# Scores of windowed and strided attention as products on quarters of the array, ahead of two expert layers

## The chip, the cores and the metric

The kernel runs on one core of one Trainium2 chip. The metric is device time in microseconds (us), from the first instruction of the program to the last. Three runs of the kernel before took 961.97, 963.13 and 961.53 us, with a median of 961.97.

TensorE (PE) multiplies a stationary operand, loaded by a weight load (PEld), with a moving operand, and writes to PSUM, which has eight banks. VectorE (DVE) and ScalarE (ACT) read PSUM and write SBUF, GpSimd (POOL) works on SBUF alone, and SyncE (SP) issues the transfers. Each engine runs its own list of instructions in order and waits on semaphores for the others.

## The reference

All of it is float32. Four batches of 576 tokens, eight heads of 64: heads 0 to 3 look at the last 32 positions, heads 4 to 7 at every position with the same remainder by 32. Then two expert layers follow, which make up most of the arithmetic.

```
scores = (q @ k.T) / 8                       # B=4, H=8, S=576, D=64
rel    = pos[:, None] - pos[None, :]
local   (heads 0-3): 0 <= rel < 32
strided (heads 4-7): rel >= 0 and both positions equal mod 32
attn   = softmax(where(mask, scores, -1e9)) @ v
x      = attn, tokens by 512                 # 2304 tokens
x      = (h - tanh(h)) @ w_out               # h = x @ w_in, 512 -> 2048 -> 512
xn     = x / rms(x) * rms_g
out    = (silu(xn @ w_gate) * (xn @ w_val)) @ w_out2      # 512 -> 1536 -> 512
```

## The kernel before, in words

The tokens are cut into nine sub-blocks, numbered `j`. Sub-blocks 0 to 3 are positions 0 to 255 of the four batches, sub-block 4 holds the last 64 positions of all four, and 5 to 8 are positions 256 to 511. They are worked in five groups, (0,1), (2,3), (4), (5,6), (7,8), with 512 columns each, 256 for the middle one. The attention of one group runs while the first expert layer of the group before it runs. For the first group there is nothing to run beside, so the program begins with attention alone.

The first expert layer has 16 steps `f`. Each step makes `ps_h` (12 products of 128 rows by 128 columns of weights, moving up to 512 columns), takes the hyperbolic tangent on ACT (`tg`), makes `g` as a high and a low part on DVE and ACT, and adds 12 products to `ps_x`. The weights come as 64-bit numbers: one weight tile is loaded as `raw` (512 KB), turned into a float by one ACT or POOL instruction (`ca`) and three of DVE (`ct`), and split into a high and a low part (`w`). `st1` walks through the weights `in 0, in 1, out 0, in 2, out 1, ...`. The second expert layer follows the same pattern with `ps_h`, `ps_m` and `ps_x`, and its weights are turned while the last group of the first layer runs.

Attention on a sub-block goes in two units of 128 rows of scores, in stages:

- `st_s`: scores into `ps_s`, then the softmax. For heads 0 to 3 (class `Local`), 64 queries of two heads form one product: the queries lie in `qz`, 128 rows by 128 columns with two blocks of zeros, so that one product on the whole array gives both heads, against 96 keys in `kT`. Four products make a unit. The first 64 positions of a batch have no keys ahead of them and use 64 keys (`wide`).
- `st_p`: the weights of the softmax are transposed on PE (`ps_p`) and copied to `pT`.
- `st_v`: the products with the values, into `ps_v`, and the copy into the expert layer's input `xs`, a high part on ACT and a low one on DVE.

Heads 4 to 7 go the same way in class `Dense` for all sub-blocks but 4: positions of equal remainder lie together, 64 keys (`k_den`, sub-blocks 0 to 3) or 128 (`k_far`, sub-blocks 5 to 8), with the queries in `qd`, zeros included. In `st_v` it makes 16 products of 32 columns, in an order of the head's numbers that the rows of `w_in` are sorted to. In sub-block 4 class `Strided` computes heads 4 to 7 with products on POOL and sums on DVE, and turns the result on DVE (`fin`, L531).

For sub-block 0 the stages draw PSUM tiles from two pools in turn, `ps_m` and `ps_h`, with two tiles each; for all later ones from `ps_m` alone, since `ps_h` belongs to the expert layer. A stage `st_s` takes one tile.

What sets the order: the string `START` names the first steps one by one (letters a to e and A to E load inputs of sub-blocks 0 and 1, `t` the masks, `w` loads a weight, `s` turns one, a digit is one stage of that sub-block, `U` is a step of the expert layer). After that the stages are spread over the steps. This gives the order in which the program is written; a scheduler then places each instruction on its engine's list by when it reckons the inputs to be ready, so lists can differ from the written order.

## Time and profile before

| | us |
|---|---|
| median of three runs | 961.97 |
| the profiled execution, its own time | 962.53 |
| its span, first instruction to last | 960.8 |
| PE busy | 929.7 (97%) |
| DVE busy | 519.9 (54%) |
| ACT busy | 346.5 (36%) |
| POOL busy | 119.6 (12%) |

The chain of work that ended last, followed back from the last instruction, is PE for 78% of the span, DVE for 11%, transfers for 5%. By tile, `ps_h`, `ps_x` and `ps_m` of the expert layers are 30%, 30% and 14%; `ps_s`, `ps_v` and `ps_p` of the attention are 2%, 2% and 1%.

How to read the rows below: a table by stretch gives, for each stretch of time, the busy time of PE, PEld, DVE, ACT and POOL with the number of instructions in brackets, then the granted clock of PE as a share of 2.4 GHz, the busy share of the transfer engines and what they moved. A row in order of time gives the start, the busy time, the engine, the line, the instruction, its operands (tile sizes of the array, then partitions by columns), how many of them are merged, and in square brackets how long the engine had idled before and for whom. Products overlap, so their cost on the path is read from start to start, not from the busy time. A float32 product appears as two instructions, so the four products of a unit's scores are "x8"; a transpose is one.

### The profile page before, as it was taken

The numbers are of one execution on the slowest core, as the hardware profiler recorded it, in microseconds if no ns is written. First come the engines' busy times: TensorE is split into PE (matmuls) and PEld (weight loads), VectorE is DVE, ScalarE is ACT, GpSimd is POOL, SyncE is SP. The second block draws the span as 40 slices with busy tenths as digits, with TensorE's granted clock in tenths as the row PEclk, the third lists the DMA queues.
The fourth block names the chain that finished last, engine by engine and source line by source line (L and its number), as shares of the span: only waits on it lengthen the run. The fifth ranks groups of instructions, "written<-read, shape, count | busy, mean of one in ns | idle before, by whom it ended". The sixth has DMA issues, their size and how long they took to land.

```text
span 960.8 us, 13712 instructions
## 1 busy us (share of the span) xinstructions
PE 929.7 (97%) x5274; PEld 779.3 (81%) x5274; DVE 519.9 (54%) x1199; ACT 346.5 (36%) x820; POOL 119.6 (12%) x147
## 2 busy tenths in 40 slices
PE   5799999999999999999899999999999999999998
PEld 5688888888999888887667778888888888888897
DVE  4899998873454433269999764254124412331212
ACT  4776654223554433244445323113111311121211
POOL 2000036760000000013334210000000000000000
PEclk9799999999999999999999999999999999999999
DMA  9936334220421200066335211101010000000100
GB/s 204 336 127 209 109 104 141 77 79 1 122 84 42 77 31 1 23 219 200 129 105 181 71 39 44 44 1 44 1 44 1 23 1 33 11 1 1 43 2 23
DMA packets 51489, 72.66 MB, mean 76 GB/s; under 512 B 24928, under 2 KB 35552, under 8 KB 51424
## 3 DMA queue, kind: packets, MB, share of 16 engines
q1 hardware_dynamic: 51424, 71.80, 24.5%
q8 instruction: 41, 0.67, 0.3%
q14 instruction: 24, 0.20, 0.1%
HBM read 62.34 MB, written 9.44 MB: 75 GB/s over the span
## 4 chain that ended last, share of the span: by engine, by line
PE 78%; DVE 11%; DMA 5%; issue 3%; POOL 1%; SPq 1%; ACT 1%; POOLq 0%; ACTq 0%
PE ps_h L111 30%; PE ps_x L111 30%; PE ps_m L111 14%; PE ps_s L111 2%; DVE ct L139 2%; DVE ct L142 2%; DVE ct L138 2%; PE ps_v L111 2%; DMA raw<-in_w_out_dram 2%; DVE w L151 1%; DMA raw<-in_w_val_dram 1%; DVE g L662 1%; PE ps_p L325 1%; DMA qz<-in_q_loc_dram 1%; DMA x<-x2d 1%
## 5 line engine op out<-in xcount | busy, mean ns | idle before, releaser
L111 PE MATMUL ps_h<-xs,w 128*128 128x512 f32 (+1 forms) x984 | 220.9, 369 | 6.2 <-DVE tg L651 6.0
L111 PE MATMUL ps_x<-g,w 128*128 128x512 f32 (+1 forms) x984 | 222.0, 368 | 0.6 <-DVE g L662 0.5
L111 PEld LDWEIGHTS ps_h<-xs,w 128*128 128x128 f32 x984 | 169.7, 190 | 37.9 <-DVE tg L651 9.2
L111 PEld LDWEIGHTS ps_x<-g,w 128*128 128x128 f32 x984 | 168.5, 188 | 31.4 <-DVE g L662 1.9
L111 PE MATMUL ps_x<-w,p 128*128 128x512 f32 x648 | 158.9, 392 | 3.5 <-DVE p L766 2.2
L111 PE MATMUL ps_m<-xn,w 128*128 128x512 f32 (+1 forms) x720 | 158.4, 368 | 0.8 <-DVE xn L745 0.8
L111 PE MATMUL ps_h<-xn,w 128*128 128x512 f32 (+1 forms) x720 | 159.0, 369 | 0.1
L763 DVE SCALAR_TENSOR_TENSOR s<-ps_m,s 128x512 f32<-128x512 f32 (+1 forms) x60 | 38.2, 637 | 221.6 <-PE ps_m L111 219.3
L111 PEld LDWEIGHTS ps_h<-xn,w 128*128 128x128 f32 x720 | 126.8, 188 | 24.8 <-DVE tg L651 0.4
L111 PEld LDWEIGHTS ps_m<-xn,w 128*128 128x128 f32 x720 | 126.0, 188 | 24.3 <-DVE xn L745 1.2
L111 PEld LDWEIGHTS ps_x<-w,p 128*128 128x128 f32 x648 | 120.4, 188 | 30.6 <-DVE p L766 3.5
L651 DVE SCALAR_TENSOR_TENSOR tg<-ps_h,tg 128x512 f32<-128x512 f32 (+1 forms) x82 | 50.9, 620 | 86.5 <-ACT tg L646 86.5
L762 ACT ACTIVATE s<-ps_h 128x512 f32<-128x512 f32 (+1 forms) x60 | 33.3, 555 | 158.9 <-PE ps_h L111 158.9
L646 ACT ACTIVATE tg<-ps_h 128x512 f32<-128x512 f32 (+1 forms) x82 | 44.5, 543 | 98.0 <-PE ps_h L111 94.3
L765 ACT CAST p<-s 128x512 fp32r<-128x512 f32 (+1 forms) x60 | 34.6, 577 | 124.1 <-DVE s L763 124.1
L657 ACT CAST g<-tg 128x512 fp32r<-128x512 f32 (+1 forms) x82 | 46.6, 569 | 51.5 <-DVE tg L651 51.4
L662 DVE TENSOR_TENSOR g<-tg,g 128x512 fp32r<-128x512 f32 (+1 forms) x82 | 55.3, 674 | 16.9 <-ACT g L657 16.6
L150 ACT CAST w<-ct 128x512 fp32r<-128x512 f32 x68 | 42.1, 620 | 45.0 <-DVE ct L142 42.5
L766 DVE TENSOR_TENSOR p<-s,p 128x512 fp32r<-128x512 f32 (+1 forms) x60 | 38.7, 645 | 25.8 <-ACT p L765 25.6
L139 DVE SCALAR_TENSOR_TENSOR ct<-ca,ct 128x512 uint32<-128x512 uint32 x68 | 52.1, 767 | 0.7
L142 DVE SCALAR_TENSOR_TENSOR ct<-raw,ct 128x512 uint32<-128x512 uint32 x68 | 51.7, 761 | 0.4
L131 ACT ACTIVATE ca<-raw 128x512 f32<-128x512 f32 x50 | 33.7, 674 | 35.1 <-DVE ct L139 18.0
(89 smaller groups left out, 723.1 us busy)
## 6 DMA issues: line engine op xcount, KB each, us to landing
raw<-in_w_out_dram SPq DMA_DIRECT2D x28, 512.0 KB, 5.8
raw<-in_w_in_dram SPq DMA_DIRECT2D x16, 512.0 KB, 8.7
raw<-in_w_gate_dram SPq DMA_DIRECT2D x12, 512.0 KB, 4.0
raw<-in_w_val_dram SPq DMA_DIRECT2D x12, 512.0 KB, 3.8
x2d<-xe SPq DMA_DIRECT2D x36, 128.0 KB, 1.9
x<-x2d SPq DMA_DIRECT2D x16, 256.0 KB, 4.2
out_dram<-o SPq DMA_DIRECT2D x16, 256.0 KB, 2.0
v<-in_v_loc_dram SPq DMA_DIRECT2D x14, 192.0 KB, 2.6
```

The costliest lines, as they stand in the source:

```text
L111: nc.tensor.matmul(out_, lhsT, rhs, start=start, stop=stop, skip_group_check=True)
L131: nc.scalar.mul(out=a, in_=hi.bitcast(F32), mul=2.0 ** -111)
L139: nc.vector.scalar_tensor_tensor(out=t, in0=a, scalar=0x80000000, in1=t, op0=ALU.bitwise_and, op1=ALU.bitwise_or)
L142: nc.vector.scalar_tensor_tensor(out=t, in0=lo, scalar=29, in1=t, op0=ALU.logical_shift_right, op1=ALU.bitwise_or)
L150: nc.scalar.copy(out=t[:, 0], in_=self.b)
L646: nc.scalar.activation(out=t, in_=h_of[g, f, a], func=ACTF.Tanh, scale=WS)
L651: nc.vector.scalar_tensor_tensor(out=t, in0=h_of.pop((g, f, a)), scalar=WS, in1=t, op0=ALU.mult, op1=ALU.subtract)
L657: nc.scalar.copy(out=t[:, 0], in_=t_of[g, f, a])
L662: nc.vector.tensor_tensor(out=t[:, 1], in0=t_of.pop((g, f, a)), in1=t[:, 0].bitcast(F32), op=ALU.subtract)
L763: nc.vector.scalar_tensor_tensor(out=s, in0=r[1], scalar=WS, in1=s, op0=ALU.mult, op1=ALU.mult)
L765: nc.scalar.copy(out=t[:, 0], in_=s)
L766: nc.vector.tensor_tensor(out=t[:, 1], in0=s, in1=t[:, 0].bitcast(F32), op=ALU.subtract)
```

## The change

- `Local.load_qk` and `Dense.load_qk`: the queries are loaded without zeros, by one transfer of 128 partitions in place of two of 64. The zero fills on POOL and DVE go.
- `st_s` of both: each head is a product of its own, on 64 rows by 64 columns of the array (a quarter). A unit has eight such products in place of four whole ones. Head `hh` of a pair uses rows `64*hh` and up, and has a PSUM tile of its own, so that a stage takes two tiles. The softmax of both classes is one function.
- The keys and values of heads 0 to 3 get 32 positions of zeros in front on the host, so that all units have 96 keys; a second mask, `mask0`, hides them. `wide` and `parts` go.
- `Dense.st_v` makes 8 products of 64 columns in place of 16 of 32, in natural head order, and the rows of `w_in` are no longer sorted.
- `Strided.fin`: four products with the identity into a PSUM tile (`ps_o`) take the place of the DVE transpose. `PR`, the size of a POOL piece, goes from 256 to 384 columns.
- `START` is another string.

```diff
-START = 'dt0AB0w00100ss100w1CDsbEU101w10csw1a1sw110w0Usw1s1e'
+START = 'tabcdewABCDEw0000s0000s0000wU1111s111s1U111s11U1'
...
-    PR = 4 * 64
+    PR = 6 * 64
...
+    def softmax(ps, sm, nm, ss, m):
+        for hh in range(2):
+            for p in range(2):
+                nc.vector.tensor_tensor_reduce(
+                    out=sm[:, hh, p], in0=ps[hh][:, p], in1=m, scale=-scale, scalar=3.0e38,
+                    op0=ALU.add, op1=ALU.min, accum_out=nm[:, hh, p:p + 1],
+                )
...
         def load_qk(self):
...
-                for hh in range(2):
-                    r = slice(64 * hh, 64 * hh + 64)
-                    nc.sync.dma_start(
-                        out=self.qz[r, x0 // 64:(x0 + n) // 64, :, r].rearrange("r u p t -> r (u p) t"),
-                        in_=q_loc[b, r, t0 // 32:(t0 + n) // 32, :],
-                    )
+                nc.sync.dma_start(
+                    out=self.q[:, x0 // 64:(x0 + n) // 64].rearrange("r u p t -> r (u p) t"),
+                    in_=q_loc[b, :, t0 // 32:(t0 + n) // 32, :],
+                )
...
         def st_s(self, i, ps_pool, ps_tag):
...
-            for u in us:
-                for p in range(2):
-                    w = self.wide(u)
-                    mm(
-                        ps[:, u - us[0], p, :w], self.qz[:, u, p, :],
-                        self.kT[:, p, self.at[u] + 96 - w:self.at[u] + 96], True, True,
-                    )
+            for p in range(2):
+                for k, u in enumerate(us):
+                    for hh in range(2):
+                        r = slice(64 * hh, 64 * hh + 64)
+                        mm(
+                            ps[hh][64 * k:64 * k + 64, p, :], self.q[r, u, p, :],
+                            self.kT[r, p, self.at[u]:self.at[u] + 96], True, True,
+                        )
...
         def st_v(self, i, ps_pool, ps_tag):
...
-                for h in range(4):
-                    r = slice(64 * (h % 2), 64 * (h % 2) + 64)
-                    for n in range(2):
-                        a = 64 * h + 32 * n
-                        mm(ps[32 * h:32 * h + 32, n, g], self.v[:, 2 * i + g, a:a + 32], pT[:, g, h // 2, r], True, True)
+                    for hh in range(2):
+                        a = 64 * (2 * p + hh)
+                        mm(
+                            ps[64 * hh:64 * hh + 64, p, g, :], self.v[:, 2 * i + g, a:a + 64],
+                            pT[:, hh, p, 64 * g:64 * g + 64], True, True,
+                        )
...
             def fin(g0, gn):
...
-                    nc.vector.transpose(
...
+                    lanes = ident.rearrange("k (p h l) -> k h p l", p=2, h=2)
+                    for c in range(gn):
+                        for hh in range(2):
+                            mm(ps[64 * hh:64 * hh + 64, :, c, :], self.o[:, c, :], lanes[:, hh], True, True)
```

Where instructions stand, before and after, at three places.

First, SP's list at the start of the program, before. `qz` and `qd` are queries, `kT` and `kd` keys, `v` and `vd` values, `raw` a weight tile.

```order
L258 DMA v<-in_v_loc_dram 96x2x256
L799 DMA tab<-in_tabs_dram 128x416
L240 DMA qz<-in_q_loc_dram 64x8x64 x2
L246 DMA kT<-in_k_loc_dram 128x2x256
...
L382 DMA kd<-in_k_den_dram 128x512
L124 DMA raw<-in_w_in_dram 128x512
L240 DMA qz<-in_q_loc_dram 64x8x64
...
L378 DMA qd<-in_q_den_dram 64x8x64
L124 DMA raw<-in_w_in_dram 128x512
L124 DMA raw<-in_w_out_dram 128x512
```

The same list after the change; the lines left out are the rest of sub-blocks 0, 1 and 2, in this order.

```order
L758 DMA tab<-in_tabs_dram 128x512
L255 DMA ql<-in_q_loc_dram 128x512
L260 DMA kT<-in_k_loc_dram 128x2x288
...
L353 DMA vd<-in_v_den_dram 64x1024
L123 DMA raw<-in_w_in_dram 128x512
L255 DMA ql<-in_q_loc_dram 128x512
...
L353 DMA vd<-in_v_den_dram 64x1024
L123 DMA raw<-in_w_in_dram 128x512
L255 DMA ql<-in_q_loc_dram 128x512
...
L123 DMA raw<-in_w_out_dram 128x512
```

The masks moved to the front, the first weight from behind one and a half sub-blocks to behind one, and the first `w_out` from behind 5136 KB to behind 6112 KB (summed over the rows of the two lists).

Second, ACT's list at the start of the program, before; `sm,ss<-sm,nm` is the exponential of the softmax.

```order
L794 ACTIVATE warm<-warm 128x1
L304 ACTIVATE sm,ss<-sm,nm 128x64 x2
L304 ACTIVATE sm,ss<-sm,nm 128x96 x2
L408 ACTIVATE sm,ss<-sm,nm 128x64 x4
...
L328 COPY pT<-ps_p 96x256
L131 ACTIVATE ca<-raw 128x512
```

The same list after the change.

```order
L753 ACTIVATE warm<-warm 128x1
L130 ACTIVATE ca<-raw 128x512
L223 ACTIVATE sm,ss<-sm,nm 128x96 x4
L223 ACTIVATE sm,ss<-sm,nm 128x64 x4
L223 ACTIVATE sm,ss<-sm,nm 128x96 x4
L223 ACTIVATE sm,ss<-sm,nm 128x64 x4
```

The first weight's `ca` moved from behind 16 exponentials and two copies to ahead of all of them.

Third, PE's list in the middle group's expert layer, where the first unit of sub-block 6 makes its scores, before.

```order
L111 MATMUL ps_x<-g,w 128x256 x11
L111 MATMUL ps_s<-kT,qz 128x96 x4
L111 MATMUL ps_x<-g,w 128x256
L111 MATMUL ps_h<-xs,w 128x256
L111 MATMUL ps_s<-kd,qd 128x128 x4
L111 MATMUL ps_h<-xs,w 128x256 x11
```

The same place after the change, with the numbers of the tiles; the two `ps_s` of a stage are the two heads of a pair.

```order
L110 MATMUL ps_s_2999<-kT_2835,ql_2834 64x96 x4
L110 MATMUL ps_x_2780<-g_2969,w_833 128x256 x3
...
L110 MATMUL ps_h_3108<-xs_1750,w_911 128x256 x12
L110 MATMUL ps_x_2779<-g_3048,w_900 128x256 x3
L110 MATMUL ps_s_3000<-kT_2835,ql_2834 64x96 x4
L110 MATMUL ps_s_3023<-kd_2864,qd_2862 64x128 x4
L110 MATMUL ps_x_2780<-g_3048,w_900 128x256 x3
...
L110 MATMUL ps_h_3163<-xs_1750,w_988 128x256 x10
L110 MATMUL ps_s_3024<-kd_2864,qd_2862 64x128 x4
L110 MATMUL ps_h_3163<-xs_1750,w_988 128x256 x2
```

Two stretches of whole products among the expert layer's became three of quarter products: the two halves of a stage, one for each tile, now stand apart.

## Rows read from the trace of the kernel before

**Rows 1.** By stretch: busy us of each engine (instructions), clock, transfer share, GB/s.

```profile
0.00:10.00 10.00, 2.18 (x10) 2.21 (x11) 0.70 (x5) 1.49 (x2) 5.89 (x15) 1.00 0.75 180
10.00:20.00 10.00, 8.72 (x43) 8.36 (x41) 6.12 (x53) 7.15 (x40) 0.00 (x0) 1.00 1.20 229
20.00:30.00 10.00, 6.26 (x119) 5.23 (x118) 7.14 (x32) 6.26 (x21) 0.00 (x0) 0.84 1.08 296
30.00:40.00 10.00, 7.71 (x46) 7.40 (x47) 8.34 (x28) 7.64 (x27) 0.00 (x0) 0.65 1.05 264
40.00:50.00 10.00, 9.33 (x142) 7.99 (x140) 9.73 (x20) 7.16 (x16) 0.00 (x0) 1.00 1.02 407
50.00:100.00 50.00, 49.83 (x351) 42.06 (x349) 48.60 (x127) 34.89 (x89) 1.04 (x2) 1.00 0.52 169
300.00:350.00 50.00, 50.00 (x351) 42.30 (x349) 23.52 (x88) 23.77 (x74) 1.05 (x2) 1.00 0.21 57
```

**Rows 2.** In order of time, PE at the start: start, busy us, what, count, idle.

```profile
7.82 3.70 PE L111 MATMUL ps_s<-kT,qz 128*128 128x64 f32 x16 [7.82 <-DMA kT<-in_k_loc_dram]
...
33.96 3.40 PE L111 MATMUL ps_h<-xs,w 128*128 128x256 f32 x13
```

**Rows 3.** In order of time, ACT at the start: first exponential, first `ca`, third `ca`.

```profile
10.11 0.35 ACT L304 ACTIVATE sm<-sm,nm 128x64 f32<-128x64 f32 x1 [7.89 <-DVE nm L296]
...
20.08 0.67 ACT L131 ACTIVATE ca<-raw 128x512 f32<-128x512 f32 x1
...
28.82 0.66 ACT L131 ACTIVATE ca<-raw 128x512 f32<-128x512 f32 x1 [1.13 <-DMA raw<-in_w_out_dram]
```

**Rows 4.** In order of time, DVE: the last input column of sub-block 1.

```profile
47.42 0.64 DVE L446 TENSOR_TENSOR xs<-ps_v,xs 128x256 fp32r<-128x256 f32 x1
```

**Rows 5.** By stretch, as rows 1: two stretches of heavy transfers.

```profile
8.00:14.00 6.00, 6.00 (x29) 6.00 (x30) 2.44 (x23) 2.02 (x11) 0.00 (x0) 1.00 1.19 190
24.00:28.00 4.00, 2.66 (x58) 2.18 (x59) 2.68 (x13) 1.91 (x9) 0.00 (x0) 0.85 1.01 386
```

**Rows 6.** In order of time, PE: expert products undisturbed, then four transposes, twice.

```profile
78.84 2.88 PE L111 MATMUL ps_h<-xs,w 128*128 128x512 f32 x12
81.56 1.98 PE L111 MATMUL ps_x<-g,w 128*128 128x512 f32 x8
...
87.01 0.60 PE L325 MATMUL ps_p<-tab,sm 128*96 128x128 f32 x4
87.45 0.60 PE L425 MATMUL ps_p<-tab,sm 128*64 128x128 f32 x4
```

**Rows 7.** In order of time, PE: scores of one unit among expert products.

```profile
361.56 1.03 PE L111 MATMUL ps_s<-kT,qz 128*128 128x96 f32 x8
362.37 2.33 PE L111 MATMUL ps_x<-g,w 128*128 128x512 f32 x9
364.53 2.89 PE L111 MATMUL ps_h<-xs,w 128*128 128x512 f32 x12
367.26 1.05 PE L111 MATMUL ps_s<-kd,qd 128*128 128x128 f32 x8
```

**Rows 8.** In order of time, PE: products with values among expert products.

```profile
382.78 2.88 PE L111 MATMUL ps_h<-xs,w 128*128 128x512 f32 x12
385.59 0.69 PE L111 MATMUL ps_v<-pT,v 96*64 96x64 f32 x16
386.20 3.02 PE L111 MATMUL ps_x<-g,w 128*128 128x512 f32 x12
389.06 2.88 PE L111 MATMUL ps_h<-xs,w 128*128 128x512 f32 x12
391.87 0.69 PE L111 MATMUL ps_v<-pT,vd 128*32 128x64 f32 x32
```

**Rows 9.** In order of time, PE: values with 64 keys, then 96, in one visit.

```profile
67.12 0.83 PE L111 MATMUL ps_v<-pT,v 64*64 64x64 f32 x16
67.88 0.73 PE L111 MATMUL ps_x<-g,w 128*128 128x512 f32 x2
```

**Rows 10.** By group: shape, count; busy us, mean ns; idle before, for whom.

```profile
L296 DVE CUSTOM_DVE_ANT_0 sm<-ps_s,tab 128x96 f32<-128x96 f32 x64 | 12.9, 253 | 2.4 <-PE ps_s L111 2.3
```

More of the change, by code (lines that the diff above doesn't have):

```diff
@@ L212, in copy @@
         return nc.scalar.copy
+    def softmax(ps, sm, nm, ss, m):
[7 more added lines that the diff above has]
+            for p in range(2):
+                nc.scalar.activation(
+                    out=sm[:, hh, p], in_=sm[:, hh, p], func=ACTF.Exp, scale=-1.0,
+                    bias=nm[:, hh, p:p + 1], accum_out=ss[:, hh, p:p + 1],
+                )
+        nc.vector.tensor_scalar_add(out=ss, in0=ss, scalar1=1.0e-9)
+        nc.vector.reciprocal(out=ss, in_=ss)
+        nc.vector.tensor_tensor(
+            out=sm, in0=sm, in1=ss.unsqueeze(3).to_broadcast(list(sm.shape)), op=ALU.mult
+        )
     class Local:
@@ L310, in st_s @@
[L310 to L314 removed]
+            softmax(ps, sm, nm, ss, m)
             self.sm[i] = sm
         def st_p(self, i, ps_pool, ps_tag):
[L318 removed]
             ps = ps_pool.tile([128, 512], F32, tag=ps_tag, name="ps_p")[0:96].rearrange(
[L320 removed]
+                "k (h p t) -> k h p t", h=2, p=2)
@@ L321, in st_p @@
             sm = self.sm.pop(i)
-            for u in range(nu):
+            for hh in range(2):
                 for p in range(2):
-                    w = self.wide(self.units[i][u])
-                    nc.tensor.transpose(ps[:w, u, p, :], sm[:, u, p, :w], ident)
-            pT = room(self.j, att, "pT", tag="pT")[0:96, :512].rearrange("k (u p t) -> k u p t", u=2, p=2)
-            for a, e, w in self.parts(i):
-                copy(self.j, 2 * i)(out=pT[:w, a:e], in_=ps[:w, a:e])
+                    nc.tensor.transpose(ps[:, hh, p, :], sm[:, hh, p, :], ident)
@@ L336, in st_v @@
             pT, v = self.pT.pop(i), self.v.pop(i)
-            for u in range(nu):
+            for u in range(2):
                 for p in range(2):
@@ L968, in lay_out @@
     r2 = row % 64
+    first = near & ((row >= 64) | (col >= 32))
     same = (r2 // 8 == c2 // 8) & (c2 <= r2)
@@ L971, in lay_out @@
     far = (r2 // 8 == c3 // 16) & (c3 % 16 <= 8 + r2 % 8)
-    near, same, far = (_np.where(m, 0.0, -BIG) for m in (near, same, far))
-    tabs = _np.concatenate([near, same, _np.eye(128), far], axis=1).astype(_np.float32)
+    masks = [_np.where(m, 0.0, -BIG) for m in (near, first, same, far)]
+    tabs = _np.concatenate(masks + [_np.eye(128)], axis=1).astype(_np.float32)
+    kp, vp = (_np.pad(a[:, :4], ((0, 0), (0, 0), (32, 0), (0, 0))) for a in (k, v))
     laid = dict(
         q_loc=q[:, :4].reshape(B, 2, 2, S // 64, 64, D).transpose(0, 2, 5, 3, 1, 4).reshape(B, 128, S // 32, 64),
-        k_loc=k[:, :4].reshape(B, 2, 2, S, D).transpose(0, 2, 4, 1, 3).reshape(B, 128, 2, S),
-        v_loc=v[:, :4].transpose(0, 2, 1, 3).reshape(B, S, 4 * D),
+        k_loc=kp.reshape(B, 2, 2, S + 32, D).transpose(0, 2, 4, 1, 3).reshape(B, 128, 2, S + 32),
+        v_loc=vp.transpose(0, 2, 1, 3).reshape(B, S + 32, 4 * D),
         q_str=lanes(q), k_str=lanes(k), v_str=lanes(v),
```

191 lines of the change are left out of this document (66 added, 125 removed).

## The prediction

> **What bounds the kernel now.** I read the table by stretch first. From 50 us on PE is busy without a gap, 49.83 of 50 us and then 50.00 of 50 [rows 1], and the chain that ended last is PE for 78% of the span. So after the start each nanosecond that PE spends more or less on attention moves the end by as much. DVE counts too until 100 us (48.60 of 50), later not (23.52 of 50) [rows 1].
>
> The start is another matter. In the first 50 us PE is idle for 15.8 us and in part of 20 to 40 us runs at the lower of its two clocks (1.2 GHz; granted share 0.84 and 0.65) [rows 1]. DVE is idle for 18.0 us in the same time (10 less each busy figure) [rows 1]. The transfer engines are full from 10 to 50 us [rows 1]. PE's first expert product starts at 33.96 us [rows 2], after a chain that passes the landing of the first `w_out`: ACT waited 1.13 us for it and began its `ca` at 28.82 us [rows 3], so it landed at about 28.4 (the start less some 0.4 us that such a chain shows between landing and start). The attention input of sub-block 1 is complete after the DVE row at 47.42 us [rows 4]; from there on PE and DVE are both full.
>
> So the forecast has two terms: the start, which waits for transfers and for DVE, and the rest, where PE's time counts.
>
> **The start.** The change loads fewer small pieces: queries come in pieces of 2 KB, not of 256 B. The stretch from 8 to 14 us, where queries with zeros, keys and values land, moves 190 GB/s at a full transfer share; the stretch from 24 to 28 us, with weights, moves 386 [rows 5]. But more stands ahead of the first `w_out` on SP's list, 6112 KB in place of 5136, since three whole sub-blocks now come first. What had moved by 28.4 us before is 180 x 10 + 229 x 10 + 296 x 8.4, 6.6 MB [rows 1]; 5648 KB with `w_out` itself are 5.8 MB, so 0.8 MB of later transfers had run beside them. After, 6624 KB (6.8 MB) and again 0.8 MB make 7.6 MB. Transfers begin to move at about 2 us (180 GB/s over 10 us [rows 1] is most of the steady rate). At 386 GB/s `w_out` lands at 21.7 us, at the mean rate of before (232 GB/s over 28.4 us) at 33; I take 300, between the two rows of 5 and near the 296 of 20 to 30 us [rows 1], since the pieces are now 1 to 2 KB for sub-blocks and 4 KB for weights: 27.3 us, 1.1 us earlier.
>
> Two things stand against a larger gain. ACT's list now has `ca` of the first weight ahead of all exponentials, so ACT waits for that weight, and the 16 exponentials of sub-block 0, the copies behind them and DVE's reciprocals wait with it. Before, the first exponential began at 10.11 us and this `ca` at 20.08 [rows 3]. Now 1952 + 512 KB (2.5 MB) are ahead, some 10 to 11 us at 300 GB/s with a start at 2, and the exponentials follow. The first scores can begin about 2 us before the 7.82 us of rows 2, since masks, queries and keys come first, but this gain ends at that wait. Second, behind `w_out` comes as much work of DVE as before: up to the last input of sub-block 1 DVE's list holds the same seven weights begun and five finished. So I carry the 1.1 us through as 1.0 us, with bounds from -6.7 us (386 GB/s) to +4.6 (232 GB/s).
>
> The zero fills on POOL are hidden now (POOL is idle after 10 us) and their removal is worth nothing beyond this. The first two units of each kind use 96 keys in place of 64, four columns of the softmax in ten more on DVE and ACT, a few hundredths of a microsecond each: nothing.
>
> **PE's time after the start.** Prices first. Twelve expert products undisturbed take 2.72 us start to start, 0.227 each [rows 6]. A unit's scores of before, eight instructions, take 0.81 us to the next start, and the nine expert products behind take 2.16 us where 2.04 is due: 0.93 us for a visit alone, 0.11 us per instruction, with 96 or 128 keys alike (1.03 and 1.05 us busy) [rows 7]. Nothing is lost ahead of it (twelve products in 2.73 us [rows 7]).
>
> Products on part of the array are dearer at the edges. The visit of 16 value products of 64 columns: the twelve expert products ahead take 2.81 us in place of 2.72, the visit 0.61, the twelve behind 2.86 [rows 8]. With 64 and then 96 keys in one visit, so one change of shape inside, it takes 0.76 [rows 9]. So a change of shape costs 0.15 us. The visit is 0.46 us of products, 58 ns for each of eight pairs side by side, and 0.09 + 0.15 + 0.14 = 0.38 us of edges.
>
> A quarter product has 64 rows and 64 columns, the shape of the first half of rows 9. With 64 keys I take 58 ns a pair. With 128 moving columns a transpose takes 0.11 us (four in 0.44 us [rows 6]), so a pair with 128 keys costs 0.11, and one with 96 about 0.085. That the time grows with the keys is my choice, by the row that has 128 moving columns; whole scores show no such growth [rows 7], and the other end is 58 ns throughout.
>
> Now the counts, from PE's list behind the scores of sub-block 1. 26 units remain. Before, they cost 26 x 8 x 0.112 = 23.3 us. After, 14 units with 96 keys, 4 with 64 and 8 with 128, of 8 pairs each, cost 9.5 + 1.9 + 7.2 = 18.5 us: 4.8 less. But visits of products on part of the array go from 22 to 59, because the scores now belong to them, and because in 22 of the 26 units the two halves of a stage stand apart, as at the third place above: 37 x 0.38 = 14.1 us. The identity products of sub-block 4 add 16 pairs, 0.9 us; values of heads 4 to 7 move from four side by side to two, 0.2; two visits with mixed keys lose their inner change, -0.3. Sum: 14.1 - 4.8 + 0.9 + 0.2 - 0.3 = **+10.1 us**. With 58 ns for all pairs the scores cost 12.1 us and the sum is +3.7. DVE's savings in sub-block 4 lie beside a full PE and count nothing.
>
> Of these products the Trainium skill speaks in "TensorEngine Tiling (Array Packing)", section Tiling Modes: at 64x64 the array is four independent tiles, whose weight loads and products run in parallel. By it, all four products of a group would share one period, the 18.5 us would halve, and the sum would be +0.9; no row here shows products on different halves of the rows side by side, and the list keeps the halves apart.
>
> **The sum.** The profiled execution took 962.53 us. -1.0 + 10.1 gives 971.6. The median of the runs is 0.56 us under the profiled execution, so 971.0 is the forecast: slower by 0.9%. Its own range is 963.5 to 977, from -6.7 and +8 to +4.6 and +11.
>
> **Rivals.** *The edges cost nothing for quarters.* The 0.38 us are read from products with values, which follow other shapes. If a quarter product among expert products had no edge, as whole scores have none ahead of them [rows 7], the 14.1 us would fall away: -1.0 - 4.0, 957. It decides from edges of 0.08 us a visit down (0.08 x 37 = 3.0, and -1.0 - 4.0 + 3.0 = -2.0). Against it: rows 8 and 9 show the edge at both ends, three times. Chance 0.13.
>
> *Quarters stream cheaper* (58 ns whatever the keys, or four side by side): +3.7 to +0.9, 964.7 to 961.9. For it: whole scores take as long with 96 keys as with 128 [rows 7]. Against: the transposes of rows 6. Chance 0.15, two thirds of it within 0.2%.
>
> *The start gains more.* Loads at 386 GB/s throughout: 965.3. The Trainium skill, "DMA: Bandwidth & Descriptors", section Specifications, asks for at least 512 B per transfer piece for full rate; rows 5 agree in kind. Chance 0.12.
>
> *PE waits for PSUM.* From sub-block 1 on a stage needs both tiles of `ps_m`, where one did before, and PE's second half waits for DVE's masked maxima of the stage before, 0.25 us each [rows 10], with the expert products queued behind it. A wait of one such row in each of 22 units adds 5.5 us: 976.5. The list puts expert products between the halves, which hides it as long as DVE is not late; DVE is free half the time after 200 us. Chance 0.12.
>
> **How the numbers follow.** Forecast 0.48, rivals 0.13, 0.15, 0.12 and 0.12. Faster is the edge rival and a few hundredths of the start's, 0.15. Same is most of the cheap stream, 0.11. Slower is the rest, 0.74. About 0.2% is what a measurement of this kernel can tell from no change. The range leaves out the edge rival and the top of the PSUM one: 961 to 978.
>
> **What would show it.** Right: single visits of eight quarter instructions with 0.15 us behind them and a slow first expert product; some 59 such visits behind the start; PE at 50 of 50 us from 50 us on; the last input of sub-block 1 on DVE at 46 to 47 us; the first `w_out` at 25 to 29 us. Wrong: four quarter products starting within 60 to 90 ns with no gap to the expert's (edges or stream), PE rows that idle for a masked maximum (PSUM), or a first expert product before 24 us with DVE full from there (start).

## The result, and the profile after

The changed kernel takes 974.26 us (median; 973.2 to 978.2) against 961.75 us, a ratio of 1.0135 [1.0104, 1.0166]. The profiled execution took 973.5 us with a span of 971.7, against 962.53 and 960.8: 10.9 us more span. The forecast of 971.0 us (961 to 978) had the sign and the size, but the 10.9 us are made up otherwise than it said.

In the experiments below one execution of 2455 us (second tile alone) and one of 1154 us (joint tiles outside the start) are slow ones and left out of the ratios.

First the table by stretch of the kernel after, columns as in [rows 1]; the last row is a short stretch in the second group.

```profile
100.00:150.00 50.00, 48.41 (x330) 38.09 (x329) 38.75 (x104) 30.72 (x74) 0.00 (x0) 0.98 0.24 69
150.00:200.00 50.00, 47.93 (x269) 37.44 (x269) 40.93 (x98) 17.10 (x44) 33.14 (x36) 0.99 0.35 115
...
148.00:151.00 3.00, 3.00 (x13) 2.27 (x11) 0.20 (x1) 0.61 (x1) 0.21 (x1) 0.50 0.87 233
```

Two of them for the kernel before, which [rows 1] left out:

```profile
100.00:150.00 50.00, 50.00 (x325) 40.86 (x324) 46.43 (x128) 29.69 (x77) 12.53 (x18) 1.00 0.31 92
150.00:200.00 50.00, 50.00 (x255) 41.06 (x254) 43.51 (x115) 17.52 (x45) 35.35 (x53) 1.00 0.35 103
```

PE is as full as before (50.00 of 50 us again from 300 to 350), but for one place: between 100 and 200 us it idles 3.7 us (50 less 48.41, 50 less 47.93), and the granted clock falls to half there (0.50 from 148 to 151 us). Nothing in the rows of before announced that.

To see where the 10.9 us arise I compare when PE starts the same piece of work in the two traces. Differences (after less before, us), each from one profiled execution; the start differs by up to 2 us between executions of kernels with the same start:

| PE starts | before | after | difference |
|---|---|---|---|
| first expert product | 33.96 | 26.60 | -7.4 |
| second unit of the expert layer | 37.08 | 36.84 | -0.2 |
| fourth unit | 49.46 | 49.50 | 0.0 |
| second group, its first unit | 144.68 | 148.25 | +3.6 |
| third group | 233.46 | 241.16 | +7.7 |
| fourth group | 299.10 | 308.56 | +9.5 |
| fifth group | 400.83 | 412.44 | +11.6 |
| last product | 956.28 | 967.22 | +10.9 |

At the fourth unit the kernel after has five products of 256 columns (0.6 us) less behind it and 0.3 us of scores more, so 0.0 there is about +0.3 of work. At the start of the second group it has twelve products (2.7 us) more behind it, so 3.6 there is +0.9. So the start gives nothing, the second group's stretch most of the loss, the third and fourth the rest.

**The start.** PE, in order of time, answering [rows 2]:

```profile
6.10 0.92 PE L110 MATMUL ps_s<-kT,ql 64*64 64x96 f32 x16 [6.10 <-DMA kT<-in_k_loc_dram]
...
26.60 1.65 PE L110 MATMUL ps_h<-xs,w 128*128 128x256 f32 x6
...
29.66 2.07 PE L110 MATMUL ps_h<-xs,w 128*128 128x256 f32 x6 [0.58 <-ACT xs L404]
```

ACT, answering [rows 3], and DVE, answering [rows 4]:

```profile
13.32 0.66 ACT L130 ACTIVATE ca<-raw 128x512 f32<-128x512 f32 x1 [11.09 <-DMA raw<-in_w_in_dram]
13.88 0.36 ACT L223 ACTIVATE sm<-sm,nm 128x96 f32<-128x96 f32 x1
...
28.46 0.66 ACT L130 ACTIVATE ca<-raw 128x512 f32<-128x512 f32 x1 [3.37 <-DMA raw<-in_w_out_dram]
```

```profile
47.58 0.63 DVE L405 TENSOR_TENSOR xs<-ps_v,xs 128x256 fp32r<-128x256 f32 x1
```

The first scores start 1.7 us earlier and the first exponential 3.8 us later (13.88 against 10.11), behind the `ca` that waits for the first weight. The first `w_out` lands when it did before, and DVE delivers the last input of sub-block 1 at 47.58 against 47.42. The first expert product is 7.4 us earlier, but its second half waits for ACT's `xs`, and by the second unit all of it is gone.

**The scores among expert products.** PE in the fourth group's stretch, answering [rows 7]: scores of one unit of both classes.

```profile
329.43 2.65 PE L110 MATMUL ps_x<-g,w 128*128 128x512 f32 x11
332.01 0.69 PE L110 MATMUL ps_v<-pT,vd 128*64 128x64 f32 x16
332.63 0.55 PE L110 MATMUL ps_s<-kT,ql 64*64 64x96 f32 x8
...
333.44 2.92 PE L110 MATMUL ps_h<-xs,w 128*128 128x512 f32 x12
336.20 1.98 PE L110 MATMUL ps_x<-g,w 128*128 128x512 f32 x8
338.11 0.30 PE L110 MATMUL ps_s<-kT,ql 64*64 64x96 f32 x2
338.13 0.33 PE L110 MATMUL ps_s<-kd,qd 64*64 64x128 f32 x2
...
339.75 2.89 PE L110 MATMUL ps_h<-xs,w 128*128 128x512 f32 x12
342.48 1.29 PE L110 MATMUL ps_x<-g,w 128*128 128x512 f32 x5
343.70 0.65 PE L110 MATMUL ps_s<-kd,qd 64*64 64x128 f32 x8
344.29 0.73 PE L110 MATMUL ps_x<-g,w 128*128 128x512 f32 x2
344.85 0.60 PE L303 MATMUL ps_p<-tab,sm 128*96 128x128 f32 x4
```

With 0.227 us for an expert product [rows 6], three costs can be read. The lone half of a stage (8 quarter instructions, 128 keys): 342.48 to 344.85 is 2.37 us for seven expert products, so 0.78. The visit at 338.11 holds two halves, one of each class, whose instructions alternate: 336.20 to 339.75 is 3.55 us for twelve products, 0.83, hardly more than one half alone. The half at 332.63 stands behind values and shares their visit: 329.43 to 333.44 is 4.01 for twelve, 1.29 for both. A lone visit of values costs 0.84 (0.46 and 0.38, read from [rows 8]), which leaves 0.45. Together the two stages cost 2.06 us, where two visits of whole products, 0.93 each by [rows 7], cost 1.87.

**Where PE stands still.** PE at the end of the first group's expert layer and the start of the second:

```profile
143.55 0.45 PE L110 MATMUL ps_s<-kd,qd 64*64 64x64 f32 x8
143.93 0.64 PE L303 MATMUL ps_p<-tab,sm 128*96 128x128 f32 x4
146.10 0.60 PE L382 MATMUL ps_p<-tab,sm 128*64 128x128 f32 x4 [1.54 <-DVE sm L229]
...
147.37 0.94 PE L110 MATMUL ps_v<-pT,vd 64*64 64x64 f32 x16
148.25 3.16 PE L110 MATMUL ps_h<-xs,w 128*128 128x512 f32 x7
151.33 0.55 PE L110 MATMUL ps_s<-kT,ql 64*64 64x96 f32 x8
...
155.24 1.43 PE L110 MATMUL ps_h<-xs,w 128*128 128x512 f32 x5
158.66 3.00 PE L110 MATMUL ps_h<-xs,w 128*128 128x512 f32 x12 [1.99 <-DVE tg L610]
161.50 0.85 PE L110 MATMUL ps_x<-g,w 128*128 128x512 f32 x3
```

DVE just before the row at 158.66 (the last of the six sums, and `tg`), and POOL:

```profile
156.64 0.55 DVE L447 TENSOR_REDUCE sc<-pr 128x6 f32<-128x384 f32 x1 [0.44 <-POOL pr L442]
...
157.92 0.68 DVE L610 SCALAR_TENSOR_TENSOR tg<-ps_h,tg 128x512 f32<-128x512 f32 x1
```

```profile
150.79 5.82 POOL L442 TENSOR_TENSOR pr<-sk,sq 128x320 f32<-128x320 f32 x6 [149.93 <-DMA sq<-in_q_str_dram]
```

The last half of the scores of sub-block 3 stands at 143.55, behind the last product of the group, and the transposes wait 1.54 us for its softmax. Before, both classes' scores of that unit stood at 122.6 to 124.3 us and its values at 139.0 to 140.7, among products. Then, from the visit of the `vd` values on (0.88 us for 0.61), PE runs at its lower level (granted share 0.50): the seven products and half-stage ahead of 151.33 take 3.08 us, against 7 x 0.227 + 0.09 = 1.68 at the upper one, 1.4 lost. Then `tg`, which frees `ps_h` and feeds the next products, stands in DVE's list behind six sums of the strided class that wait for POOL, whose six products began at 150.79 where they began at 133.73 before. PE loses 2.2 us there. All told 1.5 + 0.3 (the dear `vd` visit) + 1.4 + 2.2 = 5.4 us.

**The identity products.** Rows of one of two lone visits:

```profile
207.31 2.88 PE L110 MATMUL ps_h<-xs,w 128*128 128x512 f32 x12
210.12 0.45 PE L110 MATMUL ps_o<-tab,so 128*64 128x64 f32 x8
210.50 3.02 PE L110 MATMUL ps_x<-g,w 128*128 128x512 f32 x12
213.36 2.88 PE L110 MATMUL ps_h<-xs,w 128*128 128x512 f32 x12
```

Twelve products and the visit take 3.19 us, 0.47 over 2.72, and the twelve behind it 2.86 us, 0.14 over, so 0.61 in all. Two such and two that share a visit (0.38 and 0.54) make 2.1 us.

### The profile page after: what moved, and what is told of

It reads as the page before. It is cut to its first block, busy times and chain, and to the rows that moved or that the text cites. A ratio compares the mean times of both kernels' runs of the same rounds, so it can differ in the third digit from the quotient of the medians.

```text
span 971.7 us, 13698 instructions
## 1 busy us (share of the span) xinstructions
PE 934.3 (96%) x5322; PEld 766.9 (79%) x5322; DVE 515.4 (53%) x1162; ACT 350.0 (36%) x816; POOL 101.1 (10%) x99
## 4 chain that ended last, share of the span: by engine, by line
PE 64%; DVE 10%; issue 3%; DMA 2%; POOL 1%; ACT 0%; SPq 0%; POOLq 0%; ACTq 0%
PE ps_x L110 24%; PE ps_h L110 24%; PE ps_m L110 13%; DVE ct L138 2%; DVE ct L141 2%; DVE ct L137 2%; PE ps_s L110 1%; PE ps_v L110 1%; DVE g L621 1%; DMA raw<-in_w_gate_dram 1%; DMA raw<-in_w_out_dram 1%; DMA raw<-in_w_val_dram 1%; DVE tg L610 1%; POOL ca L132 1%; DVE w L150 1%
## 5 line engine op out<-in xcount | busy, mean ns | idle before, releaser
L110 PE MATMUL ps_h<-xs,w 128*128 128x512 f32 (+1 forms) x984 | 225.7, 373 | 8.4 <-DVE tg L610 7.3
L110 PE MATMUL ps_x<-g,w 128*128 128x512 f32 (+1 forms) x984 | 225.0, 369 | 1.7 <-DVE g L621 1.7
L110 PEld LDWEIGHTS ps_h<-xs,w 128*128 128x128 f32 x984 | 171.3, 192 | 43.6 <-DVE tg L610 10.9
L110 PE MATMUL ps_m<-xn,w 128*128 128x512 f32 (+1 forms) x720 | 158.1, 368 | 0.0
L223 ACT ACTIVATE sm<-sm,nm 128x96 f32<-128x96 f32 (+2 forms) x136 | 49.5, 365 | 33.7 <-DVE nm L217 33.4
```

The costliest lines, as they stand in the source:

```text
L110: nc.tensor.matmul(out_, lhsT, rhs, start=start, stop=stop, skip_group_check=True)
L223: nc.scalar.activation(out=sm[:, hh, p], in_=sm[:, hh, p], func=ACTF.Exp, scale=-1.0, bias=nm[:, hh, p:p + 1], accum_out=ss[:, hh, p:p + 1],)
```

## The experiments

Theories after the result: (A) the loss is PE's own, visits with edges, as predicted; (B) the loss comes from the two PSUM tiles of a stage, which make an attention unit longer, so that its end falls behind the products that should cover it; (C) the start; (D) the identity products. The expectations, written before each run, call (A) theory E (edges), (B) theory P (PSUM) and (C) S; their theory D is the order of DVE's list, tried under "The sums behind `tg`". "By the table" below means the difference to before at the starts of the groups, as in the table above.

### The second tile alone

In the kernel before, the four whole products of a stage write two `ps_m` tiles, one for each half; nothing else changes. `Dense` gets the same edit.

```diff
-            ps = ps_pool.tile([128, 512], F32, tag=ps_tag, name="ps_s")[:, :384].rearrange(
-                "q (u p t) -> q u p t", u=2, p=2)
+            ps = [
+                ps_pool.tile([128, 512], F32, tag=ps_tag, name="ps_s")[:, :192].rearrange("q (p t) -> q p t", p=2)
+                for _ in range(2)
+            ]
...
-                        ps[:, u - us[0], p, :w], self.qz[:, u, p, :],
+                        ps[u - us[0]][:, p, :w], self.qz[:, u, p, :],
```

> The kernel before, with one thing of the change: the scores of a stage go to two PSUM tiles of ps_m (one per sub-unit) instead of one; the products stay whole, the start stays as it was. Theory P (PSUM): the second tile makes the second kind's scores wait for the first kind's masked maxima, each unit of sub-blocks 2 and 3 takes one expert unit longer, and the last unit falls behind the last expert product of the group, where its stages follow one another with nothing beside them. Then PE stands still for 3 to 5 us near 140 us, the clock dips behind it, and the time is 966 to 971 us. Theory E (edges): the loss in the changed kernel is the price of products on part of the array; whole products have none, so two tiles cost nothing and the time is 961 to 963 us.

Measured: 964.83 us, 1.0028 [1.0016, 1.0040], between the two forecasts: clear of no change, but less than (B) expected, and the clock did not fall (granted share 1.00 from 100 to 200 us). By the table +0.1 at the fourth unit, +2.4 at the third group, +3.0 at the fifth. PE at the same place as above:

```profile
146.29 0.60 PE L429 MATMUL ps_p<-tab,sm 128*64 128x128 f32 x4 [0.69 <-ACT pT L330]
...
148.18 1.89 PE L111 MATMUL ps_h<-xs,w 128*128 128x512 f32 x7
```

The other wait of PE in 100 to 200 us of the same kernel (line waited for, total, times, longest):

```profile
PE ps_h L111 <- DVE tg L655: 1.1, 1, 1.1
```

The second tile by itself moves the unit's end behind the last product of the group, and the wait for `tg` appears too. That is (B) in kind, at 2.4 of the 7.7 us; with quarters the waits are longer.

### The new start alone

The kernel before with the new `START`.

```diff
-START = 'dt0AB0w00100ss100w1CDsbEU101w10csw1a1sw110w0Usw1s1e'
+START = 'tabcdewABCDEw0000s0000s0000wU1111s111s1U111s11U1'
```

> The kernel before with the changed order of the start alone (the new START string; queries still with zeros, one PSUM tile). Theories P and E both put the loss elsewhere: 960 to 964 us, PE without a stall at the end of the middle group's attention near 140 us. Rival S (start): the new order of the first loads and stages is what pushes the attention of sub-blocks 2 and 3 late, so the stall near 140 us is here too and the time is 966 to 971 us.

Measured: 970.78 us, 1.0103 [1.0063, 1.0142]. All of it lies in the first 65 us (by the table +6.7 at the second unit, +15.2 at the fourth, +14.4 at the second group and constant from there). The profiled execution, 977.5 us, overstates it: in it PE ran at the lower level, granted share 0.50, from 42.7 to 63.0 us, and the three others, with a mean share of 0.996 to 1.000 where this one has 0.989, took 969.5 to 971.7. ACT at the start:

```profile
15.12 0.66 ACT L131 ACTIVATE ca<-raw 128x512 f32<-128x512 f32 x1 [12.89 <-DMA raw<-in_w_in_dram]
17.86 0.35 ACT L304 ACTIVATE sm<-sm,nm 128x64 f32<-128x64 f32 x1 [2.09 <-DVE nm L296]
```

With the loads of before, queries in pieces of 256 B and the zero fills, the new order is bad: `ca` of the first weight begins at 15.12 us (13.32 in the changed kernel), and the exponentials wait another 2.09 us for DVE behind it. Which of the other edits makes the order harmless in the changed kernel was not tried. And PE does not stand still at 140 us: it isn't the start that makes it.

### The old start in the kernel after

The changed kernel with the `START` of before, the diff above the other way round.

> The changed kernel with the order of the start of the kernel before, nothing else. It isolates the start in the changed kernel: the prediction gave the new start -1.0 us (bounds -6.7 and +4.6), so 975.3 us by it. By the traces PE's fourth expert unit begins 0.3 us sooner than before the change: 973 to 976 us if the order of the start is neutral, with the stall near 143 us. The list now has expert products between the last stages of sub-block 3, so theory P allows 1 to 3 us less stall: 971 to 974.

Measured: 975.15 us, 1.0139 [1.0121, 1.0156], the same as the changed kernel (1.0135). By the table the stretch from the fourth unit to the third group costs 7.8 us over before, as in the changed kernel (7.7), though PE stands elsewhere: 1.95 us for `xs` ahead of 152.02, not for `tg`, with a granted share of 0.50 from 151.4 to 158.1 us. So in the changed kernel the two orders are worth the same, and (C) falls.

### The halves of a stage together

A whole product of 16 columns, the opener, writes to the second tile first, so it is this product that waits for the tile, and the 16 quarters follow it in one visit (`issue_after` places what is inside it behind the named instruction). Both classes.

```diff
+    def together(ps, quarters):
+        r = ident[:, 0:128]
+        first = mm(ps[1][:, 0, :16], r, ident[:, 0:16], True, True)
+        with tc.issue_after(getattr(first, "ins", first)):
+            second = mm(*quarters[0], True, True)
+        with tc.issue_after(getattr(second, "ins", second)):
+            for x in quarters[1:]:
+                mm(*x, True, True)
```

> The changed kernel with the two halves of a score stage kept side by side: a whole product of 16 columns on the second tile first, and all quarter products queued behind the moment when both tiles are free. Both tiles are still needed. Theory E: 22 stages lose one of two visits; by the visits of the changed kernel (0.675 us each half, 0.70 to 0.79 for a stage in one, 0.11 for the extra product) 0.55 us each, 12 us: 962 us. Theory P: half of the halves already run beside others there, so per pair of stages 2.07 us become about 1.7: 0.37 x 13 = 5 us, and the stall near 143 us with the low clock behind it stays: 968 to 970 us.

Measured: 978.23 us, 1.0155 [1.0112, 1.0198]. Both forecasts were missed. By the table +5.5 at the fourth unit, +18.3 at the third group and +19.1 at the fifth: the third and fourth groups' stretches cost 0.9 over before in place of 3.9. What was gained there was lost earlier: a stage now needs both tiles at once, the units are longer still, and PE stands 2.8 us for `tg`, 1.6 and 0.6 for `sm` and 0.6 for `nm`, with a granted share of 0.50 in two stretches (152.5 to 159.2 and 166.2 to 172.9 us). One stage's visit of PE:

```profile
322.43 3.02 PE L110 MATMUL ps_h<-xs,w 128*128 128x512 f32 x12
325.38 0.56 PE L110 MATMUL ps_s<-kT,ql 64*64 64x96 f32 x16
325.87 4.20 PE L110 MATMUL ps_h<-xs,w 128*128 128x512 f32 x17
```

16 quarter instructions, 8 pairs, in one visit with its edges: from 322.43 to the next row at 329.90 are 7.47 us, less 29 x 0.227 is 0.89. By the prediction's prices it would be 8 x 0.085 + 0.38 = 1.06 and by two visits 1.44. Both (A), the edges, and (B) are seen in this run.

### Both classes in one pair of tiles

The scores of both classes of a unit share two tiles: 32 quarter instructions in one visit behind one opener, so that a unit takes two tiles and not four. Once from sub-block 0 on, once only for sub-blocks 2 to 8, outside the start (`EA` is 2; the diff is of this one). The first also gives a unit's scores to one of sub-block 0's two pools by the unit's number.

```diff
+            if self.j >= EA and isinstance(strd[self.j][0], Dense):
+                quarters += strd[self.j][0].quarters(i, tiles, 192)
+            together(self.j, tiles, quarters)
```

> The changed kernel with the scores of both kinds of a unit in the same two PSUM tiles (one per head of a pair, both kinds side by side in its columns), all 32 quarter products in one visit behind a whole product of 16 columns. So a unit needs two tiles for two stages, as before the change. Theory P: the stall near 143 us and what follows it go (3.0 + 1.4 + 2.2 us), and a pair of score stages costs 0.38 + 0.30 + 0.44 + 0.11 = 1.2 us in place of 2.07, 11 us over 13 pairs: 956 to 959 us, faster than both kernels. Theory E: only the edges go, two visits of 0.38 us a unit, 10 us: 963 to 965 us, with the stall still there.

> As a_joint_tiles, but sub-blocks 0 and 1, whose stages make the start, keep the changed kernel's own form; only from sub-block 2 on do the scores of both kinds of a unit share two tiles, in one visit behind a whole product of 16 columns. In a_joint_tiles the fourth expert unit began 6.5 us late and all later groups together were 3.4 us shorter than in the kernel before. Theory P (the tiles and the order that follows from them): the start is the changed kernel's again, no stall near 143 us, 957 to 960 us, faster than before by 0.2 to 0.5%. Theory E (edges alone, the stall has another cause): the stall stays, 963 to 967 us.

Measured: 964.66 us, 1.0024 [1.0015, 1.0034], and 963.62 us, 1.0016 [1.0001, 1.0030], both where the expectations put the edges alone and not where (B) put them. The first loses 6.7 us in the start, where an opener waits 4.2 us for DVE's `nm` of the scores ahead of it. The second by the table: +1.2 at the fourth unit, +5.1 at the third group, +1.5 at the fifth. The wait for `sm` is gone, as (B) has it; that for `tg` is not (2.5 us), and the clock falls behind it (granted share 0.97 over 150 to 200 us). The third and fourth groups are 3.6 us *shorter* than before. PE in the fourth group's stretch of that kernel:

```profile
322.93 1.76 PE L110 MATMUL ps_x<-g,w 128*128 128x512 f32 x7
324.53 0.29 PE L110 MATMUL ps_s<-tab 128*128 128x16 f32 x2
324.67 1.18 PE L110 MATMUL ps_x<-g,w 128*128 128x512 f32 x4
325.77 0.56 PE L110 MATMUL ps_s<-kT,ql 64*64 64x96 f32 x16
326.15 0.62 PE L110 MATMUL ps_s<-kd,qd 64*64 64x128 f32 x16
326.70 0.50 PE L110 MATMUL ps_x<-g,w 128*128 128x512 f32 x1
327.04 2.90 PE L110 MATMUL ps_h<-xs,w 128*128 128x512 f32 x12
```

From 322.93 to 327.04 are 4.11 us for twelve products, so 1.39 for the scores of a whole unit with their opener, against 1.87 before and 2.06 in the changed kernel. Eight such units at 0.48 make 3.8 us, of which 3.6 are seen. This is the clearest reading of the study: the quarters are cheap, the way they stand in the list was not.

### The same with the old start

> As a_joint_late, with the order of the start of the kernel before. In the changed kernel's start PE's fourth expert unit begins at 49.1 us, in the kernel before at 49.5, so if the order of the start is worth nothing by itself this is within 1.5 us of a_joint_late. If the new order was needed by the lighter loads (theory S2), it is 3 to 9 us slower; if the old order with the lighter loads starts sooner (before, the first w_out landed at 28.4 us behind 5.1 MB, and less small pieces stand there now), it is 2 to 5 us faster.

The kernel of the last run with the `START` of before: 961.46 us, 0.9991 [0.998, 1.0001]. That is 2.2 us under the last run (963.62). With the changed kernel the two orders came out equal (0.9 us the other way), so the order of the start is worth 2 us at most, and with joint tiles rather the old one. Part of it may be the clock: the mean granted share is 0.999 to 1.000 in this run's executions and 0.987 to 0.995 in the last one's.

### Without the identity products

`fin` reads `o` in place of `ps_o`; the four products are left out.

```diff
-                    ps = ps_m.tile([128, 512], F32, tag="m", name="ps_o")[:, :2 * gn * W].rearrange(
-                        "r (p c l) -> r p c l", p=2, c=gn)
...
-                            mm(ps[64 * hh:64 * hh + 64, :, c, :], self.o[:, c, :], lanes[:, hh], True, True)
+                    ps = self.o[:, :gn, :].rearrange("r c (p l) -> r p c l", p=2)
```

> The changed kernel without the identity products that put the strided heads of sub-block 4 in place; the copies behind them read the sums as they lie, so these heads come out in the wrong places, and everything else is as it was. The prediction gave the products 0.9 us and their visits 0.38 us each. By the visits of the changed kernel, four of 0.38 to 0.58 us, 2.1 us go if PE bounds there: 971.5 to 972.5 us. If PE waits for DVE in that stretch anyway (it stood still for 2.2 us at 156 us), the gain is under 1 us: 973.5 to 974.5.

Measured: 973.28 us, 1.0112 [1.0088, 1.0137], about 1 us less than the changed kernel, with intervals that overlap. In its trace the visits of that group cost 2.3 us less, but the wait for `tg` is 2.5 us in place of 2.0 and 20 products in place of 7 run at the lower clock behind it. The 2.1 us stand in the rows, but this run doesn't confirm them: it is inconclusive.

### The sums behind `tg`

In the first step of the second group, the strided class's work on DVE is placed behind `tg`.

```diff
-        dve_g(g, f, a, e)
-        work()
+        tg = dve_g(g, f, a, e)
+        if g == 1 and f < 1:
+            with tc.issue_after(getattr(tg, "ins", tg)):
+                work()
+        else:
+            work()
```

> The changed kernel; of the strided work that goes with the first expert unit of the second group (sub-block 4), DVE's sums are queued behind that unit's own DVE step (tg), where the list had put six of them ahead of it. They wait for POOL, and POOL for keys that land at 150 us. Theory D: this queue is what makes PE stand still for 2.2 us at 156 us, and the low clock (seven products of 0.43 us in place of 0.23, 1.4 us) comes from the standing still, so 2 to 4 us go: 970 to 972.5 us. Rival: the tail of sub-block 3 at 143 us does the harm, and the sums only move the wait to the next unit: 973.5 to 975 us, with a gap of 2 us one unit later.

Measured: 971.34 us, 1.0104 [1.0087, 1.0121]. The median is 2.9 us under the changed kernel's, but the intervals overlap; by the table 1.7 us are gained up to the third group. The waits of PE in 100 to 200 us, all there are:

```profile
PE ps_p L382 <- DVE sm L229: 1.5, 1, 1.5
```

The wait for `tg` is gone and nothing came late behind it. So it was the order of DVE's list, not the sums' own time. POOL's late start alone doesn't decide: with both classes in one pair of tiles POOL had 6.2 us of its work done by 150 us, and `tg` waited longer, because there it stands behind a sum over the values (`so`, 153.10) that waits 5.0 us for POOL.

### Joint tiles, old start and the sums behind: a version faster than both

Joint tiles from sub-block 2 on, the old start and the sums behind `tg` together, and then twice with fewer openers.

> a_joint_late_start_old (961.5 us; joint tiles from sub-block 2 on, old order of the start) with the same sums queued behind the first tg of the second group. Its PE rows have gaps of 1.39, 0.38 and 0.25 us there. Theory D: these go, 958.5 to 960 us, faster than before by 0.2 to 0.35%. Rival (the wait only moves): 961 to 962 us.

Measured: 959.87 us, 0.9978 [0.9965, 0.9992]: 0.2% faster than the kernel before and 1.5% faster than the changed one. Its interval overlaps that of joint tiles with the old start alone (0.9980 to 1.0001), so what the sums add here is not shown. What is left between 50 and 440 us is one wait of PE for the identity's input,

```profile
188.75 0.34 PE L110 MATMUL ps_o<-tab,so 128*64 128x64 f32 x4 [1.69 <-DVE so L501]
```

with the lower clock behind it again (0.97 over 150 to 200 us).

```diff
-        first = mm(tiles[1][:, :16], ident, ident[:, 0:16], True, True)
-        with tc.issue_after(getattr(first, "ins", first)):
...
+        for x in quarters:
+            mm(*x, True, True)
```

> As a_joint_sums_behind without the whole product of 16 columns ahead of each visit, so nothing forces the two halves of a stage together; by the list most of them still stand in one visit and four of twelve are cut in two. 16 openers at about 0.11 us (1.7 us) go, four more visits at 0.6 us (2.4 us) come: 958.5 to 961 us, the same as a_joint_sums_behind within 1 us. If cut visits are free (no edges), 1.7 us faster than it.

> a_joint_sums_behind with the whole product of 16 columns ahead of a visit only up to sub-block 6; for sub-blocks 7 and 8 nothing forces the halves together, and the list keeps three of their four pairs of stages in one visit anyway. In the traces the group in which these two are worked took 98.7 us without it and 100.0 with it, while the groups before were shorter with it (0.9 and 1.0 us). By the rows 0.5 to 1.3 us less than a_joint_sums_behind: 958.5 to 959.5 us, 0.2 to 0.35% faster than before. If the openers hide, no change: 959.9.

Measured: without any opener 961.63 us, 0.9996 [0.9985, 1.0006]; with it only up to sub-block 6 960.99 us, 0.9983 [0.9972, 0.9994]. An opener costs 0.2 to 0.3 us (0.14 in its own row above, the rest in its neighbours), twice the 0.11 I had put down, but without it the first and the third group's stretches are 1.0 and 0.9 us longer; the fourth's, with the last attention, is 1.3 us shorter, and the second's 1.5, where PE stands 0.7 us for `so` in place of 1.7 and the clock stays up. The mixed version can't be told from that with all openers, and its reason failed: the fourth group's stretch took 100.7 us, where 98.7 was expected and 100.0 is the time with openers, because the list cut the scores of its four units into six visits there, where they make four with all openers and with none.

## Why the prediction was right, and where it was not

**The bound** was read rightly for the kernel before: PE is full from 50 us on, and there its time on attention moves the end. What I did not read from it is that this holds only while the attention's chain ends inside the group's products. The [rows 1] showed PE full; they did not show how much room each unit's end had. The sign "50 of 50 us from 50 us on" failed with it: 48.41 and 47.93 between 100 and 200 us.

**The start** (-1.0 us; 0.0 by the table, inside its bounds). The mechanism was right in its steps: earlier scores (6.10), exponentials behind the wait for the first weight, `w_out` no earlier, last input of sub-block 1 on DVE at 47.58, half a microsecond behind the forecast 46 to 47. The mis-sized term is the landing of the weights: `w_out` at 27.3 forecast, about 28.1 measured (28.46 less 0.4), and the first weight at 10 to 11 forecast, about 12.9 measured (13.32 less 0.4). The old start in the changed kernel shows the order to be worth nothing that can be told from no change (0.9 us, intervals that overlap).

**Visits** (59 forecast from the lists, 59 found, 37 more than before) and **their edges** (0.38): a lone half of a stage with 128 keys was forecast at 8 quarter instructions, 4 pairs of 0.11, and 0.38, so 0.82, and took 0.78. Right. By these prices the third and fourth groups' stretches, 23 more visits, would have cost 6.8 us more (23 x 0.38 less 1.9 for the scores), and the stretch to the third group the rest of the 10.1, 3.3.

In the prediction's sum 8 x 8 x 0.11 is 7.0 and not 7.2, which changes nothing here.

**The wrong step** is "the list keeps the halves apart", where the prediction set the four-tile rival aside. It keeps the two halves of one stage apart, but lets the second half of one class stand with the first half of the other, or with values. These run side by side: 0.83 for a visit forecast at 4 x 0.085 + 4 x 0.11 + 0.38 = 1.16. So the third and fourth groups cost 3.9 and not 6.8, and up to the third group, without the standing still, 2.3 (7.7 less 5.4) and not 3.3. Where all 32 quarter instructions adjoin, 0.93 us do (325.77 to 326.70) for what the prediction priced at 8 x 0.085 + 8 x 0.11 = 1.56 and an edge. The Trainium skill, "TensorEngine Tiling (Array Packing)", section Tiling Modes, has both sides of this: at 64x64 four tiles work in parallel, and a change of mode drains the engine. The runs agree with both, at 0.93 us for 32 and some 0.15 us for each change; what the rule gives depends on what stands next to what.

**The identity products**: forecast 16 pairs at 0.9 us, with two visits of edges inside the 37; read at 2.1 us in all. About right with their edges (0.9 + 2 x 0.38 = 1.7), but unconfirmed by the run without them.

**PE waits for PSUM** (rival, 0.12, 976.5). Its cause acted and its mechanism did not. The price I took, one masked maximum of 0.25 us in each of 22 units, is nowhere in the trace after the start. The row that answers [rows 10] (busy, mean ns; idle before, for whom) has the same mean:

```profile
L217 DVE CUSTOM_DVE_ANT_0 sm<-ps_s,tab 128x96 f32<-128x96 f32 x72 | 15.2, 252 | 17.1 <-PE ps_s L110 17.1
```

The expert products between the halves hide it, as the prediction said. But those same products make a unit last longer, and at the one place where a unit's end has nothing behind it, the end of the first group, the cost came in one piece: 5.4 us, half of the loss. The second tile alone in the kernel before makes that place (+2.4 us), joint tiles take the wait for `sm` away, and with the sums behind `tg` the wait of 2.0 us for it is gone, 1.7 us by the table. The split of the 5.4 us into its four parts is read from the rows of one execution.

**Rivals that fell:** that the edges cost nothing (0.78 for a lone half) and that the start gains more. That quarters stream cheaper fell as a result, 964.7 to 961.9, but stands as a mechanism wherever quarters adjoin.

**The sum, as measured:** start 0.0; to the third group 5.4 of standing and low clock and 2.3 of PE's own; third and fourth groups 3.9; behind the fifth -0.7, for which I have no cause. 10.9 us. The forecast's 9.1 us is near it by luck: 3.9 us too much of PE's own cost (10.1 for 6.2) stand against 5.4 us of standing that it didn't have.

Open: why POOL's first strided products came 17 us later is read from SP's list (`sk` and `sq` issue at 145.0 us behind the eight loads of the next sub-blocks; before, at 129.2), not tried by itself. And no run separates the fall of the clock from the wait ahead of it.

## What to carry to other kernels

A product on a part of the array is cheap when its neighbours on the list are such products and dear among whole ones, so count visits and what adjoins in each, not instructions; two stages that share tiles can go in one visit. A second buffer for a stage is paid in the length of the chain: look where a pipeline's last unit ends at the border of a group, since a full engine in a table by stretch says nothing of the room there. And on an engine with slack, an instruction that frees a resource for the bound engine belongs ahead of those that wait for a third engine.

## What the runs showed of the hardware

- The granted clock stayed at 1.00 behind stands of PE of 0.7 and 1.1 us (second tile alone), behind 1.99 us in the changed kernel (twelve products took 2.84 us, 158.66 to 161.50), and behind 1.71 us in the kernel before, in the row below; the fifth group has a like stand, 1.5 to 1.7 us, in every run, and none fell there. Behind stands of 1.54, 1.69 and 2.5 us products ran at the lower level, 1.2 GHz (granted share 0.50 from 148 to 151 us; an expert product of 512 columns at about 0.43 us for 0.227), and the 1.54 us cost 1.4 us more. So the length of a stand alone does not decide. Ahead of the 1.54 and 1.69 us PE had last done transposes, or products on parts of the array; ahead of the 1.71 and 1.99 us, but of the 2.5 us too, whole products. No run tests whether that is the reason.

```profile
460.88 2.88 PE L111 MATMUL ps_x<-g,w 128*128 128x512 f32 x12
465.47 3.01 PE L111 MATMUL ps_h<-xs,w 128*128 128x512 f32 x12 [1.71 <-DVE tg L651]
```

- Quarters of different stages, on the upper and the lower rows, run side by side (starts at 338.11 and 338.13): 8 + 8 instructions in one visit cost 0.83 us, 8 alone 0.78. 16 with 96 keys in one visit took 0.38 us from start to start (325.77 to 326.15).
- A whole product of 16 columns among whole ones costs 0.2 to 0.3 us, about as much as one of 512 columns.
